# First layer of a fused attention and expert kernel: first w_in row blocks loaded among pair 3, seven column groups open at once, a narrow float16 warm-up

## Chip, cores, metric

One core of one Trainium2 chip. The metric is device time in microseconds (us) for one execution. Each kernel is compared with the kernel before by runs on the same chip in the same rounds.

## The reference, cut to what matters

```python
kv  = einsum('bhsd,bhse->bhde', k, v)           # 8 batches, 8 heads, 576 rows, 64 columns
out = einsum('bhsd,bhde->bhse', q, kv)
x   = out / sqrt(mean(out*out) + 1e-6) * g_norm # then (8*576) x 512
h   = x @ w_in                                  # 512 x 2048: the first layer
g   = h * (1 / (1 + exp(-1.702 * h)))           # the gate
y   = g @ w_out                                 # 2048 x 512: the second layer
```

## The kernel before

TensorE does the attention of batch b+1 between the matmuls of the two layers of tile b. Only for batch 0 is there nothing to hide behind. Its 8 heads are handled as four pairs. For each pair the kernel transposes q, forms the key-value product, multiplies the two ("out"), squares on ScalarE, sums on TensorE, takes ln and exp on ScalarE ("rs") and applies the factor on VectorE. That gives one of the four row blocks (ko) of xT. The first layer of tile 0 needs row block ko of xT and of w_in for its matmul (ko, fo); there are 16 column groups fo, and a group's sum stays in a PSUM buffer until all four row blocks are in.

```python
    GROUP = 6
    ...
    for c in range(1, NPAIR):                 # loads of batch 0, pairs 1 to 3
        for n in "qkv":
            early_load(n, 0, c, c + 1)
    load_w_in(0, 4, 0, 2)                     # column groups 0..3, row blocks 0 and 1
    load_w_in(0, 4, 2, KO)
    load_w_in(4, GROUP)
    load_w_in(GROUP, 10)
    load_w_in(10, FO)
    ...
    for _ in range(3):                        # warm-up of TensorE, float32
        nc.tensor.matmul(idle_ps, zeros[:, 0:P], zeros, start=True, stop=True)
    a0.q(0)
    busy(2)                                   # two idle 512-column matmuls
    a0.kv(0)
    ...
    a0.q(3)
    a0.kv(3)
    a0.sums(2)
    a0.apply(1)
    a0.out(3)
    a0.rs(2)
    a0.apply(2)
    busy(1)
    d0 = Hidden(0)
    for fo in range(4):
        d0.mm(0, fo, ...)
        if fo == 2:
            a0.ss(3)
            a0.apply(3)
    for ko in range(1, KO):
        for fo in range(4):
            d0.mm(ko, fo)
    for fo in range(4, GROUP):
        for ko in range(KO):
            d0.mm(ko, fo, ps_o, "o")
    for fo in range(GROUP):
        d0.gate(fo)
```

After this the other column groups run one by one, each through one of three buffers of the pool `ps_h`, and the second layer follows.

## Time and profile before

| what | value | where from |
|---|---|---|
| time, median of 3 | 287.08 us (286.64 to 287.28) | runs |
| span of the profiled run | 285.0 us | profile page |
| first matmul of the first layer | 14.24 us | TensorE timeline |
| last row block of xT ready | 16.78 + 0.75 = 17.53 us | VectorE timeline |
| second layer starts | 29.00 us | TensorE timeline |
| from there to the end | 285.0 - 29.0 = 256.0 us | the two rows above |

From 29 us on TensorE has no hole, so 256.0 us is what all later work costs, and a change of the first 29 us moves the end one for one. The lines are in the prediction below.

### The profile page before, as it was taken

To read this page: it belongs to the slowest core of one execution; us is meant where nothing else is said; L and a number is where in the kernel's file an instruction comes from. 1 tells how busy PE (TensorE), PEld (TensorE's weight loads), DVE (VectorE), ACT (ScalarE), POOL (GpSimd) and SP (SyncE) were. 2 spreads that over 40 slices of the span, in tenths; PEclk is the share of its full clock that TensorE was granted. 3 is DMA by queue.
4 is the path that set the end of the run, shared out by engine and by line. 5 is a ranking of instruction groups with operands and counts; after the bars stand their busy time and mean duration, and the time that the engine had idled before them with its cause. 6 is when DMAs were issued, how large, how long until landed. Compare 5 with 4: busy or idle time off the path is not lost.

```text
span 285.0 us, 4335 instructions
## 1 busy us (share of the span) xinstructions
PE 278.8 (98%) x1707; PEld 134.9 (47%) x1707; DVE 119.2 (42%) x231; ACT 156.2 (55%) x273; POOL 57.2 (20%) x82
## 2 busy tenths in 40 slices
PE   7899999999999999999999999999999999999995
PEld 3444554455445544554455445544454444444443
DVE  2650566527661657157713852286327400110001
ACT  2697439766575645574468536763666365016400
POOL 8931551111211121112011401130002100000000
PEclk9999999999999999999999999999999999999999
DMA  8999999999589356953798279925401410011022
GB/s 176 198 207 204 207 246 235 201 240 179 122 165 254 61 145 161 245 85 71 218 200 152 38 215 198 188 39 184 83 2 37 119 65 2 0 67 80 2 74 74
DMA packets 54070, 38.76 MB, mean 136 GB/s; under 512 B 31219, under 2 KB 50931, under 8 KB 53923
## 3 DMA queue, kind: packets, MB, share of 16 engines
q0 software_dynamic: 14960, 15.58, 33.5%
q1 hardware_dynamic: 38688, 22.39, 30.6%
q10 hardware_dynamic: 402, 0.52, 0.6%
q8 instruction: 13, 0.21, 0.3%
q14 instruction: 7, 0.05, 0.1%
HBM read 36.73 MB, written 9.44 MB: 162 GB/s over the span
## 4 chain that ended last, share of the span: by engine, by line
PE 93%; DMA 3%; POOL 3%; issue 0%; DVE 0%
PE hT L436 43%; PE o L473 42%; DMA w_in_sb<-in_moe_w_in_dram 3%; PE kvp L225 3%; PE outR L289 2%; PE oh L505 1%; POOL qraw L91 1%; POOL kraw L91 1%; POOL vbuf L91 1%; PE ss L337 1%; PE q L414 0%; PE outT L268 0%; PE outT L257 0%; POOL w_in_sb L168 0%; POOL ident L154 0%
## 5 line engine op out<-in xcount | busy, mean ns | idle before, releaser
L473 PE MATMUL o<-w_out_sb,gT 128*128 128x512 f16 x560 | 130.7, 379 | 0.0
L445 ACT ACTIVATE gT<-hT 128x512 f16<-128x512 f32 x144 | 84.7, 599 | 76.8 <-PE hT L436 76.5
L436 PE MATMUL hT<-xT,w_in_sb 128*128 128x512 f16 x512 | 116.5, 379 | 0.1
L436 PEld LDWEIGHTS <-w_in_sb 128*128 128x128 f16 x576 | 54.3, 98 | 63.1 <-DMA w_in_sb<-in_moe_w_in_dram 1.6
L473 PEld LDWEIGHTS <-gT 128*128 128x128 f16 x560 | 52.9, 98 | 56.4
L483 DVE COPY osb<-o 128x512 f32<-128x512 f32 x20 | 13.8, 690 | 62.3 <-PE o L473 62.3
L321 POOL TENSOR_TENSOR x<-xr,g_all 128x512 f16<-128x512 f32 x12 | 15.3, 1272 | 71.2 <-DVE xr L314 47.2
L216 DVE COPY kpad<-kraw 64x576 f16<-64x576 f16 x56 | 25.0, 446 | 1.7 <-DMA kraw<-in_k_dram 0.4
L300 DVE TENSOR_REDUCE sum<-sq 128x8 f32<-128x512 f16 x24 | 15.8, 679 | 19.9 <-ACT sq L297 19.9
L238 DVE CAST kvb<-kvp 64x128 f16<-64x128 f32 x28 | 8.1, 288 | 36.5 <-PE kvp L225 36.3
L314 DVE TENSOR_TENSOR xr<-outR,sum 128x512 f32<-128x512 f32 x24 | 15.5, 686 | 11.1 <-ACT sum L311 11.1
L112 POOL DMA_DIRECT2D kraw<-in_k_dram x16 | 10.0, 625 | 48.2 <-DVE kpad L216 42.3
L112 POOL DMA_DIRECT2D vbuf<-in_v_dram x16 | 9.7, 610 | 34.1 <-PE kvp L225 29.3
L321 DVE TENSOR_TENSOR x<-xr,g_all 128x512 f16<-128x512 f32 x12 | 15.2, 1267 | 0.7
L297 ACT ACTIVATE sq<-outR 128x512 f16<-128x512 f32 x24 | 13.6, 591 | 2.0 <-PE outR L289 1.6
L225 PEld LDWEIGHTS <-kpad 128*128 128x128 f16 x252 | 11.1, 98 | 6.5 <-DVE kpad L216 0.2
L436 PE MATMUL hT<-x_rem,w_in_sb 128*128 128x512 f16 x64 | 14.0, 379 | 0.0
L277 ACT ACTIVATE sq<-outT 128x512 f16<-128x512 f32 (+1 forms) x16 | 7.7, 481 | 11.0 <-PE outT L257 9.5
L483 ACT COPY osb<-o 128x512 f32<-128x512 f32 x15 | 8.7, 582 | 6.3 <-PE o L473 6.3
L310 ACT ACTIVATE sum<-sum,eps_t 128x16 f32<-128x16 f32 x12 | 3.7, 308 | 15.0 <-DVE sum L300 14.9
L225 PE MATMUL kvp<-vbuf,kpad 128*128 128x64 f16 x252 | 11.9, 193 | 0.0
L339 ACT ACTIVATE ln<-ss,eps_t 128x512 f32<-128x512 f32 (+1 forms) x16 | 9.4, 585 | 3.4 <-PE ss L337 3.4
(65 smaller groups left out, 140.7 us busy)
## 6 DMA issues: line engine op xcount, KB each, us to landing
qf<-in_q_dram SPq DMA_DIRECT2D x5, 1024.0 KB, 8.7
out_dram<-osb SPq DMA_DIRECT2D x10, 512.0 KB, 2.9
kraw<-in_k_dram POOLq DMA_DIRECT2D x12, 288.0 KB, 7.5
vbuf<-in_v_dram POOLq DMA_DIRECT2D x12, 288.0 KB, 5.4
w_out_sb<-in_moe_w_out_dram POOLq DMA_DIRECT2D x3, 512.0 KB, 14.8
out_dram<-osb SPq DMA_DIRECT2D x6, 192.0 KB, 5.6
qf<-in_q_dram POOLq DMA_DIRECT2D x1, 1024.0 KB, 12.2
out_dram<-osb SPq DMA_DIRECT2D x1, 1024.0 KB, 3.8
```

What stands on the lines that cost most here:

```text
L112: nc.gpsimd.dma_start(out=raw[n][l * PH : (l + 1) * PH, c0:c1, 0 : NH * D], in_=srcs[n][b].rearrange("(c l) (p j) d -> l p c (j d)", l=2, ...
L216: nc.vector.tensor_copy(out=kpad[r, c, :, l * D : (l + 1) * D], in_=kraw[r, c, 0 : NH * D].rearrange("p (j d) -> p j d", j=NH),)
L225: nc.tensor.matmul(self.kvp[:, c, :], kpad[:, c, j, :], vbuf[:, c, j * D : (j + 1) * D], start=(j == 0), stop=(j == NH - 1),)
L297: nc.scalar.activation(sq, t, AFT.Square)
L300: nc.vector.tensor_reduce(out=self.sum2[:, j % 2, :], in_=sq.rearrange("p (h d) -> p h d", h=H), op=ALU.add, axis=mybir.AxisListType.X,)
L314: nc.vector.tensor_mul(xr[:, i], self.o[j + i].rearrange("p (h d) -> p h d", h=H), s2[:, i, :].unsqueeze(2).to_broadcast([P, H, D]),)
L321: (nc.vector if i else nc.gpsimd).tensor_mul(self.x16[:, j + i, :].rearrange("p (h d) -> p h d", h=H), xr[:, i], g_all.unsqueeze(1).to_bro ...
L339: nc.scalar.activation(ln[:, 0:n], t[:, 0:n], AFT.Ln, bias=eps_t, scale=1.0 / D)
L436: nc.tensor.matmul(self.h[fo], w_in_sb[:, ko, fo * P : (fo + 1) * P], self.x[:, ko], start=(ko == 0), stop=(ko == KO - 1),)
L445: nc.scalar.activation(self.gT[:, fo, :], self.h[fo], AFT.Gelu_apprx_sigmoid)
L473: nc.tensor.matmul(os[mo], gT[:, fo, mo * P : (mo + 1) * P], w_out_sb[:, fo, :], start=(fo == 0), stop=(fo == FO - 1),)
L483: copy(osb[:, mo, :], os[mo])
```

## The change

Its intent is to start the first layer earlier. Small pieces of w_in are to be there when the first row block of x is, seven groups instead of six give TensorE work while it waits for the last row block, and the warm-up no longer needs a float32 tile. Later slots are moved to suit. The core of the diff:

```diff
-    GROUP = 6
+    GROUP = 7
...
-    zeros = const.tile([P, SM], F32)
-    nc.vector.memset(zeros, 0.0)
...
             early_load(n, 0, c, c + 1)
-    load_w_in(0, 4, 0, 2)
-    load_w_in(0, 4, 2, KO)
-    load_w_in(4, GROUP)
-    load_w_in(GROUP, 10)
-    load_w_in(10, FO)
+            if c == NPAIR - 1 and n != "v":
+                ko = "qk".index(n)
+                load_w_in(0, 4, ko, ko + 1)
+    load_w_in(0, 4, 2, 3)
+    load_w_in(4, 6, 0, 3)
+    load_w_in(6, GROUP, 0, 3)
+    load_w_in(0, GROUP, 3, KO)
+    load_w_in(GROUP, 9)      # and (9, 11), (11, 13), (13, FO)
...
-    for _ in range(3):
-        nc.tensor.matmul(idle_ps, zeros[:, 0:P], zeros, start=True, stop=True)
+    for _ in range(64):
+        nc.tensor.matmul(
+            idle_ps[:, 0:D], kvb[1][:, 0, :], kvb[1][:, 0, 0:D], start=True, stop=True
+        )
+    busy(4)
...
     a0.q(3)
-    a0.kv(3)
-    a0.sums(2)
     a0.apply(1)
-    a0.out(3)
-    ...
+    d0 = Hidden(0)
+    d0.mm(0, 0)
+    a0.sums(2)
+    a0.rs(2)
+    d0.mm(0, 1)              # and (0, 2), (0, 3)
+    for fo in range(4):
+        d0.mm(1, fo)
+    a0.apply(2)
+    a0.kv(3)
+    d0.mm(2, 0)
+    a0.out(3)
+    for fo in range(1, 4):
+        d0.mm(2, fo)
+    a0.ss(3)
+    a0.apply(3)
+    for fo in range(4, GROUP):
+        for ko in range(KO - 1):
+            d0.mm(ko, fo, ...)
+    for fo in range(GROUP):
+        d0.mm(KO - 1, fo)
...
     (cut and told in words from here on)
-    (k, v, w_out of tile 1 in turn)     -> (w_out blocks 8 to 11 before v)
-    (key-value products of tile 1 at steps 27, 28, 42, 43)  -> (36, 37, 46, 47)
-    (outputs at 32, 35, 50, 53)         -> (41, 43, 52, 53); loads of tiles 2 and 3 a little later,
     and the first matmuls of the later tiles take the first four groups in the order 0, 3, 1, 2
```

More of the change, by code (lines that the diff above doesn't have):

```diff
@@ L177 @@
             early_load(n, 0, c, c + 1)
-    load_w_in(0, 4, 0, 2)
-    load_w_in(0, 4, 2, KO)
-    load_w_in(4, GROUP)
-    load_w_in(GROUP, 10)
-    load_w_in(10, FO)
+            if c == NPAIR - 1 and n != "v":
[6 more added lines that the diff above has]
+    load_w_in(GROUP, 9)
+    load_w_in(9, 11)
+    load_w_in(11, 13)
+    load_w_in(13, FO)
     nc.scalar.preload_act_table_set("natural_log_exp_and_others")
@@ L450, in dense @@
         if group and t:
-            order = [(ko, fo) for part in (range(4), range(4, group)) for ko in (0, 1) for fo in part]
+            order = [(ko, fo) for part in ((0, 3, 1, 2), range(4, group)) for ko in (0, 1) for fo in part]
             order += [(ko, fo) for ko in range(2, KO) for fo in range(group)]
@@ L592 @@
     a0.q(3)
+    a0.apply(1)
+    d0 = Hidden(0)
[3 more added lines that the diff above has]
+    d0.mm(0, 1)
+    d0.mm(0, 2)
+    d0.mm(0, 3, ps_a, "att")
+    for fo in range(4):
+        d0.mm(1, fo)
+    a0.apply(2)
     a0.kv(3)
-    a0.sums(2)
-    a0.apply(1)
+    d0.mm(2, 0)
     a0.out(3)
-    a0.rs(2)
-    a0.apply(2)
-    busy(1)
-    d0 = Hidden(0)
-    for fo in range(4):
-        d0.mm(0, fo, *((ps_h, "hT") if fo < 3 else (ps_a, "att")))
-        if fo == 2:
-            a0.ss(3)
-            a0.apply(3)
-    for ko in range(1, KO):
-        for fo in range(4):
-            d0.mm(ko, fo)
+    for fo in range(1, 4):
+        d0.mm(2, fo)
+    a0.ss(3)
+    a0.apply(3)
     for fo in range(4, GROUP):
-        for ko in range(KO):
-            d0.mm(ko, fo, ps_o, "o")
+        for ko in range(KO - 1):
+            d0.mm(ko, fo, *((ps_o, "o") if fo < 6 else (ps_a, "att")))
+    for fo in range(GROUP):
+        d0.mm(KO - 1, fo)
     for fo in range(GROUP):
@@ L616 @@
     load_w_out(4, 8)
-    for c in (0, 2):
-        load_half("k", 1, c, c + 2)
-        load_half("v", 1, c, c + 2)
-        if c == 0:
-            load_w_out(8, 12)
-        else:
-            load_w_out(12, 14)
-            load_w_out(14, FO)
+    load_half("k", 1, 0, 2)
+    load_w_out(8, 10)
+    load_w_out(10, 12)
+    load_half("v", 1, 0, 2)
+    load_half("k", 1, 2, NPAIR)
+    load_half("v", 1, 2, NPAIR)
+    load_w_out(12, 14)
+    load_w_out(14, FO)
     load_q(2, nc.gpsimd)
@@ L660 @@
                 at2(9 + 3 * c, of(1, "q", c))
-                at2((21, 21, 33, 33)[c], of(1, "pack_k", c))
-                at2((27, 28, 42, 43)[c], of(1, "kv", c))
-                o = (32, 35, 50, 53)[c]
+                at2((21, 21, 38, 38)[c], of(1, "pack_k", c))
+                at2((36, 37, 46, 47)[c], of(1, "kv", c))
+                o = (41, 43, 52, 53)[c]
                 at2(o, of(1, "out", c))
                 if c == NPAIR - 1:
-                    at2(46, load_kv, 2)
-                at2((38, 46, 56, 59)[c], of(1, "ss", c))
-                at2((38, 46, 56, 59)[c], of(1, "apply", c))
+                    at2(48, load_kv, 2)
+                at2((45, 48, 56, 58)[c], of(1, "ss", c))
+                at2((48, 51, 56, 60)[c], of(1, "apply", c))
         elif b < B:
@@ L679 @@
             if t + 2 < B:
-                at1(f0, load_q, t + 2)
-                at1((10 if t == 1 else 9) + 4, load_kv, t + 2)
+                at1(12 if t == 1 else f0, load_q, t + 2)
+                at1((11 if t == 1 else 9) + 4, load_kv, t + 2)
             for c in range(NPAIR):
                 at1(f0, of(b, "pack_k", c))
-                at1((10 if t == 1 else 9) + c, of(b, "kv", c))
+                at1((11 if t == 1 else 9) + c, of(b, "kv", c))
             at2(6, nc.scalar.preload_act_table_set, "natural_log_exp_and_others")
```

## The prediction

> **What bounds the kernel now.** I read the page first (busy shares), then the chain that ended last, then the first 30 us engine by engine, then the DMA landings there.
>
> ```profile
> PE 278.8 (98%) x1707; PEld 134.9 (47%) x1707; DVE 119.2 (42%) x231; ACT 156.2 (55%) x273; POOL 57.2 (20%) x82
> ...
> PEclk9999999999999999999999999999999999999999
> DMA  8999999999589356953798279925401410011022
> ```
>
> TensorE is busy 98% of the span, and the DMA engines are full for the first quarter. Busy is not the same as useful, so the chain, limited to the first 30 us, decides:
>
> ```profile
> 8.01 0.72 POOL w_in_sb L168
> 8.73 7.80 DMA w_in_sb<-in_moe_w_in_dram
> 16.53 0.05 issue
> 16.58 5.48 PE hT L436 x24
> 22.06 0.12 PE outT L268 x4
> 22.17 6.99 PE hT L436 x32
> ```
>
> The chain follows a load of w_in until 16.53, and then nothing but TensorE. From 22 us on its pieces hold 0.216 us per 512-column matmul with no hole worth naming. As a check I count the matmuls after 29.0 us, where the second layer starts: 560 x 0.216 (second layer) + 512 x 0.216 (first layer of tiles 1 to 8) + about 21 us of small ones (252 key-value products at 0.029, 96 row products at 0.056, sums, transposes, the split last tile) = 252.5 us. The chain needs 281.6 - 29.0 = 252.6 us for them. So **only what happens before 29 us can be won**, or new stalls created after it. The TensorE timeline there:
>
> ```profile
> 13.79 0.39 PE L257 MATMUL outT<-qT,kvb 128*128 128x512 f16 x1
> 14.02 0.38 PE L560 MATMUL idle<-kvb 128*128 128x512 f16 x1
> 14.24 0.82 PE L436 MATMUL hT<-xT,w_in_sb 128*128 128x512 f16 x3
> 14.98 0.38 PE L337 MATMUL ss<-sq,ones 128*128 128x512 f16 x1
> 15.20 6.86 PE L436 MATMUL hT<-xT,w_in_sb 128*128 128x512 f16 x29
> 21.89 0.28 PE L268 MATMUL outT<-qT,kvb 128*128 128x64 f16 x4
> ```
>
> The first layer of tile 0 starts at 14.24 and its first 32 matmuls (8 column groups x 4 row blocks) are issued by 21.89. They and one sum need 33 x 0.216 = 7.13 us; they got 7.65. About 0.5 us is lost. The list of waits says to what (columns: us in total, times, longest):
>
> ```profile
> PEld L436 <- DMA w_in_sb<-in_moe_w_in_dram: 1.6, 4, 0.6
> ```
>
> And ScalarE beside it:
>
> ```profile
> 15.40 0.69 ACT L339 ACTIVATE ln<-ss,eps_t 128x512 f32<-128x512 f32 x1
> 16.11 0.63 ACT L345 ACTIVATE rs<-ln 128x512 f32<-128x512 f32 x1
> 16.76 1.28 ACT L445 ACT_TABLE_LOAD   x1
> 18.06 3.77 ACT L445 ACTIVATE gT<-hT 128x512 f16<-128x512 f32 x7
> 22.09 0.60 ACT L445 ACTIVATE gT<-hT 128x512 f16<-128x512 f32 x1 [0.27 <-PE hT L436]
> ```
>
> The last normalised block (xT of pair 3) is ready at 17.53, the gate table follows at once, and by 22.09 the gates wait for TensorE and not the other way.
>
> **DMA landings.** From the issue times and the latencies asked one issue at a time: q, k, v of pair 3 land at 11.45, 12.2 and 12.9; the w_in pieces at 14.2, 16.5, 17.5, 20.05 and 23.8. In steady state a 144 KB piece takes 0.75 us and 256 KB about 1.3 us (some 200 KB per us). The POOL timeline also shows that issue number n stands until issue n-8 has landed (the second key half waits for the second w_in piece, the third w_out piece for the last w_in piece), so eight loads are in flight at most.
>
> [...]
>
> **The change part by part.**
>
> Warm-up: three float32 matmuls (5.06 us, ending near 6.5) become 64 narrow ones[...] and four wide ones[...], starting 0.2 us earlier since one memset of 0.48 is gone.[...] The key-value product of pair 0 waits for the cast of v, which ends at 7.59 because v lands at 6.9. So this part is worth 0.
>
> Loads: two pieces of 128 KB come before k and v of pair 3, about 0.65 us each. k of pair 3 lands near 12.9, v near 14.3; the pieces land near 12.1, 13.5, 15.0 (row block 2), 16 and 16.5 (groups 4 to 6), 17.5 to 18 (row block 3 of all seven).
>
> TensorE order, with the durations above (ln 0.69, rs 0.63, square 0.59, apply 0.75, product to kvb 0.29, 0.38 from a matmul's start to its result). Until the transposes of pair 3 at 11.96 all is as before. Then: xT0 ready 12.56, so row block 0 starts at 12.62; its four matmuls and the sum of pair 2 end at 13.8. xT1 is ready at 14.20 (rs ends 13.41, apply 0.75), so row block 1 runs 14.26 to 15.12: **0.45 us stall**. Key-value of pair 3: 15.12 to 15.4, and its copy to kvb follows apply of pair 2 (14.76 to 15.51) on VectorE: 15.6 to 15.9. Row block 2 starts with xT2 at 15.57; the output of pair 3 at 15.93; three more to 16.8. Square 16.35 to 16.94, sum 16.99, ln to 18.11, rs to 18.76, apply to 19.55. Meanwhile 9 matmuls of groups 4 to 6; group 5 takes the buffer of that sum and waits for ln: 18.16, **0.3 us stall**. Row block 3 starts at 19.6, 7 x 0.216 to 21.11, group 7 to 21.98. Before: 21.89. So **the front is a tie, +0.1 us**: the first layer starts 1.6 us earlier, but the last block of x comes 2.0 us later (19.55 against 17.53), because the output of pair 3 now stands behind eight matmuls and two loads.
>
> Gates: table load 18.78 to 20.06, then one per 0.48 us (the spacing in the group above). Gate 7 ends at 20.06 + 7 x 0.48 + 0.60 = 24.0. Group 10 needs the buffer of group 7 (three buffers), and TensorE would be there at 21.98 + 0.12 + 2 x 0.864 = 23.83. **Stall 0.2 to 0.3.** The smaller pieces of w_in take away the wait of under 0.1 at 23.8. Start of the second layer: 29.0 + 0.1 + 0.25 - 0.1 = 29.25.
>
> Later slots of tile 0: the w_out pieces for blocks 8 to 11 come before v, so key-value products move from step 27 to 36. Walking through the 64 steps: v lands near 37.2 and is used at 38.1; w_out 12 to 13 lands at 41.3 as now and is used near 42.4; the second normalised output of tile 1 ends within 0.2 us of its use. All just fit: 0. The moved loads of tiles 2 and 3: 0.
>
> Sum: +0.25 us, that is 287.3.
>
> **The rivals.** (1) *The stalls vanish and the earlier start is kept.* With no stall the same work from 12.3 ends at 20.3 rather than 21.9: at most -1.6. But w_out 14 to 15 lands at 42.7 now and is used at 43.3, in a stream of loads that is full from the start, so some 0.6 to 0.9 is all that can be kept: about 286.3. For it speaks that the later slots were all moved back relative to the loads, which is only needed if TensorE gets ahead of them. Against it, the chain of pair 3 worked out above. (2) *Loads take over*: the small pieces run below 200 KB per us, or v of pair 3 lands a microsecond later; each 0.1 us of that goes straight into the last xT and into the end: 288. The before has one such skew (256 KB landing in 2.3 us). (3) *A later slot stalls*: key-value of tile 1 before v is there, 0.3 to 0.8 us: 287.8. (4) *Warm-up fails*:[...] some 0.3 us of transposes and products longer, 287.4.
>
> **Range and chances.** My sum gives 287.3, rival 1 286.3; I give the sum somewhat more weight but not all, because the moved slots look measured: 287.0. The three runs of before spread over 0.6 us, and the stalls are known to 0.3 each: 286.0 to 287.9. 2% is 5.7 us; all that can be won is 1.6, and nothing here adds 5, so within 2% at 0.98, faster 0.005, slower 0.015.
>
> **What would show it right or wrong.** Right: first hT matmul near 12.6; stalls before row block 1 and row block 3; last xT of tile 0 near 19.5; table load near 18.8; gates back to back until group 10 and a short wait there; second layer from 29.0 to 29.5; no hole after. Wrong: last xT before 18.5, or a second layer that starts before 28.5 (rival 1); a wait for w_in or v of over 0.3 us in the front (rival 2); a hole between 36 and 47 us (rival 3); narrow matmuls or transposes at twice their duration after 6.5 us (rival 4).

The sum of the forecast came to +0.25 us, that is 287.3: +0.1 for the front, +0.25 for the gate wait (put at 0.2 to 0.3), -0.1 for the smaller pieces of w_in, 0 for the warm-up and for the later slots. The marks stand for what no profile of the kernel before showed: the durations of the new warm-up's matmuls and the end of the warm-up that followed from them, an allowance for the narrowest w_in piece (not a term of the sum), and how long rival 4 lasts. The 0 for the warm-up rests on the cast of v (7.59) and on my estimate that the new warm-up is over by then; that ScalarE and VectorE work in program order is an assumption of the schedule. The first profile of the changed kernel has the 64 narrow matmuls 0.053 us apart, the four wide ones 0.43 apart, and the end of both at 6.58.

## The result, and the profile after

The changed kernel took 287.44 us (median of six, 287.18 to 289.17), the kernel before 286.96 (six runs). The ratio is 1.0023 with an interval of 1.0 to 1.0047. Repeated in five more rounds it was 287.37 against 286.93, ratio 1.0016 (1.0004 to 1.0028). The change costs about 0.45 us; that is within 2%.

The profile that came with the first result is of the slowest of the six runs, 289.17 us. Its page has a line that differs from the one of before (the clock granted to TensorE in tenths, 40 slices of 7.2 us):

```profile
PEclk9979999999999999999999999999999999999999
```

The third slice is at 7. The clock records say that it was half from 13.90 to 17.31 us. (Where the expectations below name times of the clock or of instruction packets, such as 14.14 to 17.55 or 14.6, these were counted from a zero 0.24 us earlier than that of the timelines; in the text all times have the zero of the timelines.) In the TensorE timeline of the same run seven 512-column matmuls take 3.1 us (14.04 to 17.16) instead of 1.5:

```profile
14.04 3.19 PE L440 MATMUL hT<-xT,w_in_sb 128*128 128x512 f16 x7
...
17.16 0.43 PE L378 MATMUL kv<-vbuf,kraw 96*64 96x64 f16 x12
```

The other five runs took 287.2 to 287.7, so this is not what the median is made of.

### The profile page after: what moved, and what is told of

It reads as the page before. It is cut to its first block, busy times and chain, and to the rows that moved or that the text cites. A ratio compares the mean times of both kernels' runs of the same rounds, so it can differ in the third digit from the quotient of the medians.

```text
span 287.4 us, 4460 instructions
## 1 busy us (share of the span) xinstructions
PE 280.9 (98%) x1768; PEld 137.5 (48%) x1768; DVE 119.0 (41%) x230; ACT 155.9 (54%) x273; POOL 61.0 (21%) x88
## 4 chain that ended last, share of the span: by engine, by line
PE 91%; ACT 4%; DMA 2%; POOL 1%; issue 0%; DVE 0%
PE hT L440 42%; PE o L477 41%; PE kvp L229 3%; DMA vbuf<-in_v_dram 2%; PE outR L293 2%; ACT gT L449 1%; PE oh L509 1%; PE ss L341 1%; ACT ln L343 1%; ACT sq L281 1%; POOL qraw L91 0%; ACT L449 0%; ACT rs L349 0%; POOL kraw L91 0%; PE q L418 0%; PE outT L261 0%
## 5 line engine op out<-in xcount | busy, mean ns | idle before, releaser
L440 PE MATMUL hT<-xT,w_in_sb 128*128 128x512 f16 x512 | 118.5, 383 | 0.3 <-ACT gT L449 0.2
L440 PEld LDWEIGHTS <-w_in_sb 128*128 128x128 f16 x576 | 55.0, 98 | 63.9 <-issue 3.4
## 6 DMA issues: line engine op xcount, KB each, us to landing
w_out_sb<-in_moe_w_out_dram POOLq DMA_DIRECT2D x4, 256.0 KB, 10.3
```

The costliest lines, as they stand in the source:

```text
L440: nc.tensor.matmul(self.h[fo], w_in_sb[:, ko, fo * P : (fo + 1) * P], self.x[:, ko], start=(ko == 0), stop=(ko == KO - 1),)
```

## The experiments

Twelve kernels ran, each with five rounds. All gave correct results. Each call has its own runs of the kernel before (medians 286.93, 286.88, 286.93) and was on another chip: e1 to e4, e5 to e8 and e9 to e12 ran together. A difference of 0.2 to 0.4 us between a kernel and e1_again of another call is therefore a hint, which its profile has to bear out; where I could, I read it from the profiles. The table has landmarks from every profile. "Front" is the start of the second layer; "rest" is the span minus it.

| kernel | time, median (range) | ratio to before | first kv product | first-layer start | last xT | front | rest |
|---|---|---|---|---|---|---|---|
| before | 286.96 | 1 | 7.64 | 14.24 | 17.53 | 29.00 | 256.0 |
| changed, first profile (half clock) | 287.44 | 1.0023 | 7.67 | 13.26 | 21.63 | 31.41 | 256.0 |
| e1_again | 287.37 (287.22 to 287.68) | 1.0016 | 7.52 | 13.18 | 19.83 | 29.61 | 256.0 |
| e2_old_warm | 287.62 (287.12 to 288.23) | 1.0022 | 7.87 | 12.84 | 19.85 | 29.63 | 256.0 |
| e3_warm_only (half clock) | 287.64 (287.30 to 288.37) | 1.0025 | 7.42 | 15.13 | 19.13 | 30.52 | 256.0 |
| e4_kv_early (half clock) | 287.19 (286.96 to 288.20) | 1.0013 | 7.73 | 13.59 | 20.51 | 30.44 | 256.0 |
| e5_wide_warm | 286.72 (286.66 to 287.17) | 0.9994 | 7.79 | 14.45 | 17.73 | 29.41 | 256.0 |
| e6_pair_first | 286.76 (286.44 to 288.25) | 1.0003 | 7.12 | 13.96 | 18.46 | 28.60 | 256.0 |
| e7_old_slots | 287.02 (286.83 to 287.29) | 1.0001 | 7.07 | 12.80 | 19.45 | 29.23 | 255.9 |
| e8_gate_buf | 287.07 (286.71 to 287.23) | 1.0000 | 7.76 | 12.73 | 19.74 | 29.19 | 256.1 |
| e9_all_three | 286.58 (286.28 to 287.87) | 0.9995 | 7.78 | 13.77 | 18.47 | 28.34 | 256.3 |
| e10_after_wide | 287.25 (286.56 to 288.12) | 1.0003 | 7.47 | 12.60 | 20.56 | 30.35 | 256.1 |
| e11_group6 | 287.80 (287.50 to 288.08) | 1.0027 | 7.36 | 13.21 | 19.86 | 30.02 | 256.0 |
| e12_more_instr | 287.41 (287.06 to 287.80) | 1.0013 | 8.17 | 15.06 | 18.27 | 29.66 | 256.0 |

Two readings come before the single runs. First, the rest is 255.9 to 256.3 in all fourteen profiles: whatever these kernels gain or lose, they do it before the second layer. Second, the first key-value product starts anywhere from 7.1 to 8.2 us, in most profiles because the first v lands at different times from run to run. A single profile is therefore uncertain by some tenths.

### e1_again: the changed kernel once more

No edit.

> The changed kernel, unaltered, to get a second profile. In the first profile (289.17 us, when its other five runs took 287.2 to 287.7) the granted clock fell to half from 14.14 to 17.55 us. Theory 1 (the sum of stalls of my prediction): the typical run has no half-clock stretch, takes 287.4, the second layer starts between 29.2 and 29.7, the last xT of tile 0 is ready near 19.5, group 10 of the first layer waits 0.2 to 0.3 us for a gate. Theory 2 (half clock is the loss): every run of the changed kernel has a half-clock window after 7 us and without it would be at 286 or below; then the profile shows matmuls 0.43 us apart again.

The second profile has full clock from 6.77 us on. The first part of its page (busy us, share of the span, instructions of each engine) hardly differs from that of before, 98% for TensorE again, which is why the busy share is no help here:

```profile
PE 278.9 (98%) x1768; PEld 137.0 (48%) x1768; DVE 118.9 (42%) x230; ACT 155.9 (55%) x273; POOL 61.0 (21%) x88
```

Its TensorE timeline answers to the one of before in the prediction:

```profile
13.18 0.39 PE L440 MATMUL hT<-xT,w_in_sb 128*128 128x512 f16 x1 [0.66 <-DMA w_in_sb<-in_moe_w_in_dram]
...
13.62 1.67 PE L440 MATMUL hT<-xT,w_in_sb 128*128 128x512 f16 x7
15.22 0.38 PE L378 MATMUL kv<-vbuf,kraw 96*64 96x64 f16 x12
16.00 0.38 PE L440 MATMUL hT<-xT,w_in_sb 128*128 128x512 f16 x1 [0.40 <-DVE xT L355]
16.22 0.38 PE L261 MATMUL outT<-qT,kvb 128*128 128x512 f16 x1
...
17.28 0.38 PE L341 MATMUL ss<-sq,ones 128*128 128x512 f16 x1
17.50 4.92 PE L440 MATMUL hT<-xT,w_in_sb 128*128 128x512 f16 x20
22.25 0.28 PE L272 MATMUL outT<-qT,kvb 128*128 128x64 f16 x4
...
24.43 5.34 PE L440 MATMUL hT<-xT,w_in_sb 128*128 128x512 f16 x24 [0.17 <-ACT gT L449]
```

The first layer starts 1.06 us earlier than before (13.18 against 14.24). But the product of pair 3 (line L378) starts at 15.22 instead of 13.02, behind the eight matmuls, and so the mark of 32 first-layer matmuls, the four small ones at 22.25, comes 0.36 later than the 21.89 of before. The eight matmuls after that mark need 1.73 us and would leave TensorE free at 24.1; the next starts at 24.43, a hole of 0.33. The chain that ended last shows the two halves of this (start, length, what; before it was TensorE alone from 16.58):

```profile
17.28 0.39 PE ss L341
...
17.70 0.69 ACT ln L343
...
18.41 0.63 ACT rs L349
...
19.06 1.28 ACT L449
...
20.36 4.03 ACT gT L449 x8
...
24.43 5.34 PE hT L440 x24
```

From 17.70 to 24.39 the chain runs through ScalarE: ln, rs, table load, eight gates. What ends last in that stretch has changed from TensorE to ScalarE, because the sum of the last pair comes 2.3 us later (17.28 against 14.98). Most of this is a load: v of pair 3 lands at 14.75 in e1 and at 12.88 before, so 1.87 of the 2.20 us by which its product is later are the landing, and only 0.33 its place in the program. What follows: theory 1, the sum of stalls, describes the typical run; a half-clock stretch is an extra that single runs have.

### e2_old_warm and e3_warm_only: the warm-up in both directions

e2 is the changed kernel with the old warm-up (and its zeros tile); e3 is the kernel before with the new one.

```diff
# e2: on the changed kernel                    # e3: on the kernel before, the reverse
-    for _ in range(64): (64-column matmul)
-    busy(4)
+    for _ in range(3):
+        nc.tensor.matmul(idle_ps, zeros[:, 0:P], zeros, start=True, stop=True)
```

> The changed kernel with the old warm-up (a zeros tile and three float32 matmuls). Theory 1: the warm-up is worth nothing, so within 0.2 us of the changed kernel, 287.4. Theory 2: the narrow warm-up matmuls are what leaves the array in a state from which it falls back to half clock; with the old ones no run shows the 1.5 us longer time, median 286.5 to 287.2.

> The kernel before with the new warm-up alone. Theory 1: 287.0 as before, within 0.2. Theory 2 (narrow warm-up costs clock): 287.3 or more, or single runs 1.5 us longer than the rest.

e3 is a miss for theory 1: the warm-up alone costs the kernel before 0.7 us in the median. Two of its six runs (288.26 and 288.37) have a mean granted clock of 0.994, the sign of a half-clock stretch; the mean of the four others, 287.50, is still 0.5 above that of before (286.97). So something costs time at full clock. It shows in the DMA queues between 10.5 and 12 us (queue: packets, MB, share of 16 engines). First the kernel before, then e3:

```profile
q0 software_dynamic: 412, 0.30, 130.6%
```

```profile
q0 software_dynamic: 402, 0.29, 127.1%
q8 instruction: 1, 0.02, 4.0%
```

One packet of 16 KB on a queue of kind instruction: 4.0% of 16 engines over 1.5 us is 0.96 us of a single engine; the packet records have it from 10.75, 0.949 us long. The kernel before has the same packet at 14.41. The loads show what goes with it. In e3 k of pair 3 lands 1.63 us after q of pair 3 (11.20 and 12.83), where 0.7 to 0.75 is the usual step; v of pair 3 lands at 13.25. TensorE waits for it, 1.21 us against 0.62 us before (bracket at the end; before, then e3):

```profile
13.02 0.38 PE L374 MATMUL kv<-vbuf,kraw 96*64 96x64 f16 x12 [0.62 <-DMA vbuf<-in_v_dram]
```

```profile
13.39 0.53 PE L372 MATMUL kv<-vbuf,kraw 96*64 96x64 f16 x12 [1.21 <-DMA vbuf<-in_v_dram]
```

In the kernel before, the packet meets the second piece of w_in instead: 256 KB land 2.3 us after the piece ahead of them, where 1.3 is usual. That is the "skew" my prediction mentions without a cause. In twelve of the fourteen profiles the load that lands 2.0 to 2.6 us after the start of the first such packet is 0.6 to 1.5 us later than its usual step; the exceptions are the first profile of the changed kernel and e12 (about 0.2).

Why it moves: the queue's kind is all that the trace says of the packet; that it brings TensorE's instructions is a reading of mine, and so is the name "16 KB fetch" in the expectations below. Its counts and times agree with that reading: the page of each kernel with the 64 narrow matmuls has 14 such packets, that of every other kernel 13, and in the first ten profiles TensorE had executed 221 to 304 matmuls and weight loads when the first packet within the loads came, be it at 10.6 or at 15.4 us. The new warm-up has 136 of them (64 + 64 and 4 + 4) where the old shows as twelve; by that reading the packet comes earlier.

e2 also missed both expectations in part: 287.62, no better. Its packet comes at 14.72 and the first w_in piece lands at 12.23 instead of 13.13. From the first key-value product to the second layer its profile has 21.76 us against 22.09 in e1; but that product itself is 0.35 later (7.87), since the float32 matmuls held the first transposes until 6.96, 0.46 later than in e1. So the last xT is ready at the same time, 19.85.

### e5_wide_warm: few instructions, same length

```diff
-    for _ in range(3):                       # on the kernel before; zeros tile removed
-        nc.tensor.matmul(idle_ps, zeros[:, 0:P], zeros, start=True, stop=True)
+    busy(12)                                  # 24 instructions
```

> The kernel before with twelve wide float16 matmuls as its warm-up: cold time as long as the new one (12 x 0.43 = 5.1 us), no zeros tile, but 24 TensorE instructions instead of 136. The warm-up alone had cost 0.5 us (287.64 against 286.93), which I had put at 0. Theory A[...]: a 16 KB packet of kind instruction took 0.95 us on one DMA engine, at 14.6 us in the kernel before and at 10.8 to 11.7 with the narrow warm-up, where the key and value loads of pairs 2 and 3 queue behind it; with few instructions it goes back to 14 to 15 us, v of pair 3 lands at 12.9 and the time to 287.0. Theory B (narrow matmuls or the missing memset leave the clock worse): 287.5 as with the narrow ones or single runs with a half-clock window.

286.72, ratio 0.9994 (0.9981 to 1.0007): the loss of e3 is gone, with the same missing memset and float16 operands as in e3. The packet is at 15.38, and the wait for v of pair 3 is back:

```profile
13.23 0.38 PE L372 MATMUL kv<-vbuf,kraw 96*64 96x64 f16 x12 [0.68 <-DMA vbuf<-in_v_dram]
```

Theory A stands: what the narrow warm-up cost the kernel before goes with the place of the instruction packet. (e5 changes the width and the number of the matmuls at once; what singles out the packet is the late k in e3 and the wait for v, 0.59 us longer there than before, which is the loss.) No run of e5 had a lower clock. The two medians in the expectation differ by 0.71; 0.5 is the difference at full clock. The 0.43 us per matmul in the expectation is the spacing of the four wide ones in the first profile of the changed kernel.

### e12_more_instr: only the number of instructions

```diff
     a0.q(0)
-    busy(2)            # on the kernel before, warm-up unchanged
+    narrow(22)         # 22 matmuls of 64 columns
...
-    busy(2)
+    narrow(16)
```

> The kernel before, its warm-up kept, with the four wide idle matmuls around the first key-value product replaced by 38 narrow ones of the same total time: 68 more TensorE instructions. Theory A (fetch position): the 16 KB fetch moves from 14.6 to 11.5 to 12.7 us, k or v of pair 3 or the first w_in piece lands up to 0.9 us late, 287.2 to 287.6. Rival (the narrow warm-up cost something else, such as clock or memset): fetch position is harmless, 286.9.

287.41 and none of the six runs below 287.06, as theory A expects, but the profile does not bear it out. The packet came at 12.98, later than I had said, and met only the first w_in piece; from the first key-value product to the second layer it took 21.49 us (before: 21.36). Its excess lies ahead of that, in a v that landed later (the product starts at 8.17). This run is inconclusive.

### e4_kv_early and e6_pair_first: where pair 3 stands

e4 moves the product of pair 3 ahead of row block 1. e6 moves it ahead of row block 0 too, with the sum of pair 2 first, and loads q, k, v of pair 3 before any w_in.

```diff
# e4                                   # e6
     d0.mm(0, 3, ps_a, "att")               a0.q(3)
+    a0.kv(3)                          +    a0.sums(2)
+    d0.mm(1, 0)                       +    a0.rs(2)
+    a0.out(3)                         +    a0.kv(3)
-    for fo in range(4):                    a0.apply(1)
+    for fo in range(1, 4):                 d0.mm(0, 0)
         d0.mm(1, fo)                  +    a0.out(3)
     a0.apply(2)                            (row blocks 0 and 1)
-    a0.kv(3)                               a0.apply(2)
     d0.mm(2, 0)                       +    a0.ss(3)
-    a0.out(3)                              (row block 2)
+    a0.ss(3)                               a0.apply(3)
     (cut here)                             (cut here)
```

> The changed kernel with the key-value product of pair 3 put before row block 1 instead of after it, and its output and sum accordingly earlier; loads unaltered. Theory 1 (the last xT is late because that product stands behind eight matmuls): last xT ready near 18.6 instead of 19.5, 0.5 to 0.8 us faster than the changed kernel, some 286.7. Theory 3 (v of pair 3 lands so late that its place in the program is irrelevant, loads bind): the product starts after 15 us in either order and the time stays within 0.2 us of the changed kernel.

> The changed kernel with q, k and v of pair 3 all loaded before w_in (the first row blocks right after), and the product and output of pair 3 put before row blocks 0 and 1. Theory 1 (the early w_in pieces and the place of pair 3 make the last xT late): last xT ready near 18.0 instead of 19.8, second layer from 28.0 to 28.7, 286.2 to 286.7. Rival: the first layer then waits for w_in as in the kernel before, last column groups late, 287.0 or more.

e4 gained 0.2 us in the median (287.19 against 287.37), less than expected; five of its runs are at 286.96 to 287.35 and the profiled one fell to half clock, so its last xT cannot be compared. By its numbers theory 3 is the one that came true: v of pair 3 landed at 15.28, the product started at 15.83, and the time stayed within 0.2 us. e6 has the last xT at 18.46 instead of 19.83, the second layer at 28.60 instead of 29.61, and a median of 286.76. The product of pair 3, now early in the program, still starts as soon as v has landed (13.34, against 14.75 in e1):

```profile
13.38 0.38 PE L377 MATMUL kv<-vbuf,kraw 96*64 96x64 f16 x12 [0.37 <-DMA vbuf<-in_v_dram]
```

That landing is 1.41 us earlier and the last xT 1.37, so the gain comes with the order of the loads; the place in the program alone is what e4 shows. From the sum of pair 3 to the mark of 32 matmuls TensorE has no wait,

```profile
16.12 5.34 PE L439 MATMUL hT<-xT,w_in_sb 128*128 128x512 f16 x24
```

and only the gate wait is left after it (the next 32 matmuls take 7.34 us, where e8 needs 7.07). Two of e6's six runs (288.25 and 288.08) have the lower clock, which is why its ratio is 1.0003. What follows: the early w_in pieces and the place of pair 3 together cost the changed kernel about 0.6 us (287.37 - 286.76; 0.8 with the means of full-clock runs, 287.41 and 286.60). The seven groups and split row blocks are not to blame; e6 has them.

### e7_old_slots: the later slots and loads as before

```diff
-  kv at (36, 37, 46, 47), out at (41, 43, 52, 53), ...   # on the changed kernel
+  kv at (27, 28, 42, 43), out at (32, 35, 50, 53), ...   # and the load order, all as before
```

> The changed kernel with the load order after the front and all later slots of tiles 0 to 2 as in the kernel before. Theory 1 (the moved slots are worth 0): 287.4 within 0.2. Rival: the old slots stall where the new ones do not, 287.7 or more; or the new ones cost, 287.1 or less.

The rest is 255.9 us with the old slots and 256.0 with the new: they are worth 0 with this front. The median is 0.35 lower than that of e1, outside my 0.2, so by the time alone the rival (287.1 or less, the new slots cost) came true; in its profile the first key-value product starts at 7.07, 0.45 earlier than in e1, and from there to the second layer it took 22.16 us against 22.09. I cannot say whether the old order of later instructions has a part in that or only the time at which the first loads landed in those runs.

### e8_gate_buf: the wait for gate 7

```diff
                 for ko in range(KO):
-                    hid.mm(ko, fo)
+                    hid.mm(ko, fo, *((ps_o, "o") if t == 0 and fo == 10 else (None,)))
```

> The changed kernel with column group 10 of tile 0 in a buffer of the other pool, free since gate 4. Theory 1: the wait of group 10 for gate 7 (0.33 us in the second profile) goes, second layer 0.3 earlier, 287.1. Rival: group 11 then waits for the same gate or the w_in piece binds there, 287.4.

287.07, 0.3 less than e1. The hole is gone: from the mark of 32 matmuls to the second layer the profile has 7.02 us (22.17 to 29.19) against 7.36 in e1 (22.25 to 29.61), and the TensorE timeline has 32 matmuls in one piece where e1 has 8 and 24:

```profile
22.28 7.07 PE L440 MATMUL hT<-xT,w_in_sb 128*128 128x512 f16 x32
```

### e11_group6: without the seventh group

```diff
-    GROUP = 7
+    GROUP = 6
-    load_w_in(6, GROUP, 0, 3)
```

> The changed kernel with six column groups open instead of seven. Theory: the last xT stays at 19.8, and three matmuls (0.65 us) that filled the wait for it now come after it, while the gate wait of 0.33 goes: 287.6 to 287.9. Rival: the seventh group fills nothing that would be idle and only makes the gate wait: 287.1.

287.80, 0.4 more than e1. The last xT is unmoved (19.86), and TensorE now stands before it:

```profile
19.91 3.18 PE L439 MATMUL hT<-xT,w_in_sb 128*128 128x512 f16 x14 [0.64 <-DVE xT L354]
```

0.64 us is the three matmuls. The second layer starts 0.41 later than in e1 (30.02 against 29.61). So the seventh group is worth 0.4 us net here: it fills a wait that the rest of the change has made.

### e10_after_wide and e9_all_three: the repairs

e10 is the changed kernel with `busy(12)` as its warm-up. e9 is e6 with that warm-up and with the buffer of e8.

> The changed kernel with twelve wide matmuls as warm-up and nothing else altered. Theory (fetch): the 16 KB fetch goes back to 14 to 16 us, the first piece of w_in lands near 12.3 instead of 13.1, no half-clock window; 287.0 to 287.2, since the late last xT and the gate wait stay. Rival: the warm-up costs nothing here because that late xT hides it, 287.4.

> The changed kernel with the three repairs together: pair 3 before w_in and its product early (as the kernel of that name), twelve wide matmuls as warm-up, column group 10 in the free buffer. In all ten profiles so far the span minus the start of the second layer is 255.9 to 256.1, so only that start counts. Theory: second layer at 28.0 to 28.4, 286.0 to 286.4, no run with a half-clock window. Rival (loads cap it): w_out blocks 12 to 15 land at 41.7 and 43.1 whatever the front does, TensorE waits for them in steps 48 to 52, and the time stays at 286.5 or above.

e10 gave 287.25 (286.56 to 288.12), hardly less than e1. The packet went back to 14.57 as expected, but in the changed kernel something urgent is loading then too. In the profiled run, the slowest of the six, it met row block 2 of w_in, which landed at 16.68, 2.0 us after the v ahead of it (14.69) where 128 KB usually take 0.65:

```profile
16.73 0.39 PE L440 MATMUL hT<-xT,w_in_sb 128*128 128x512 f16 x1 [1.30 <-DMA w_in_sb<-in_moe_w_in_dram]
```

e9 has the front at 28.34, within the expected range, and its best runs are at 286.28 to 286.40, half a microsecond under before. But the rest has grown to 256.26. In its chain the first key-value product of tile 1 waits for v (landed at 37.57), a block of w_out (43.01) and a sum take a little more:

```profile
37.63 0.08 issue
37.71 0.42 PE kvp L228 x9
...
43.02 0.03 issue
43.05 0.38 PE o L476
...
45.37 0.30 PE ss L340
```

The wait for v is what e6 does not have: of e9's lead of 0.26 us over e6 at the second layer, 0.03 is left at 46.75 us. So the loads begin to cap a faster front, as rival 1 said. The expected 286.0 to 286.4 was missed. And e9 had one run at lower clock (287.87) and one at 287.63 without: median 286.58, ratio 0.9995 (0.997 to 1.002). No kernel is shown to beat the one before.

### The half-clock stretch

Where a profile has it, it lasts 3.41 us and starts 6.83 us after the clock first went to full (before: the clock records begin, at full, at 6.05; first profile: at 7.07). The second half of these 6.83 us is a window in which TensorE waits for loads. Busy time of the engines in that window and the next, changed kernel, first profile (columns: stretch, length, then busy time and instruction count of PE, PEld, DVE, ACT, POOL; clock, DMA share, GB/s):

```profile
10.49:13.90 3.41, 2.34 (x41) 1.28 (x41) 1.86 (x4) 2.67 (x6) 3.00 (x5) 1.00 1.24 180
13.90:17.31 3.41, 3.41 (x14) 1.06 (x14) 1.50 (x2) 1.65 (x3) 3.32 (x5) 0.50 1.31 171
```

and e1, which kept its clock:

```profile
10.18:13.59 3.41, 2.46 (x41) 1.32 (x41) 2.10 (x5) 3.17 (x6) 2.29 (x5) 1.00 1.24 189
```

The other two that fell (e3, e4) had 2.20 and 2.10 us of TensorE work in that window, and the kernel before had 2.65. But e10 kept its clock through a later window with 2.27:

```profile
15.62:19.04 3.42, 2.27 (x9) 0.89 (x10) 0.17 (x1) 1.21 (x2) 2.27 (x4) 1.00 1.40 197
```

So little work in that window goes with the fall, and a fixed limit on busy time as the profile counts it does not explain it. Counting runs with a mean clock of 0.993 or 0.994: 6 of 45 runs of the kernels with the 64 narrow matmuls, 2 of 61 of those without (one of 33 of the kernel before, one of six of e9). That is a hint that the narrow warm-up makes the fall more frequent; with such counts it is not shown.

## Why the prediction was right or wrong

The time on record was 287.0 with a range to 287.9; it came out at 287.44. Its own sum, 287.3, was nearer than the number I made of it.

**Only what is before 29 us counts: right.** The rest is 256.0 us before and after, and within 0.3 in every experiment.

**The front is a tie, with an earlier start and a later last xT: right in mechanism, mis-sized by 0.3.** I had the start at 12.62, the last xT at 19.55, the 32-matmul mark at 21.98; e1 has 13.18, 19.83 and 22.25, and a second layer at 29.61 where I had 29.25. The term that was off is the landing of the first w_in piece, 12.1 in my list and 13.1 in e1, where the 16 KB packet (11.08 to 12.02) comes just ahead of it: it lands 1.58 us after q of pair 3, and 128 KB usually take 0.65. It delays the sum of pair 2 from about 12.95 (implied by my 15.51) to 13.40 and with it xT of pair 2 from 15.51 to 15.95. Where that piece landed at 12.23 (e2) the start is at 12.84. The 0.45 us stall before row block 1 shows as 0.28 in e2 and is absent in e1, where row block 0 came late enough; the stall of group 5, put at 0.3, is there: the 20 matmuls from 17.50 to 22.25 need 4.32 us and got 4.75, and the first matmul of group 5 stands until 18.43, just after ln ends at 18.39 (0.28), the rest being the wait for the last xT. The product behind "eight matmuls and two loads" is right too, but the loads weigh more than the matmuls: that e6 moves both and gains 0.6, and e4 the program alone and gains 0.2, shows the cause.

**The gate wait, 0.2 to 0.3: right.** 0.33 in e1; taking it away gains 0.3 (e8).

**The warm-up is worth 0: wrong.** This is the step that failed. I followed the TensorE path only. There the warm-up does cost nothing, since the first key-value product starts at 7.52 in e1 and at 7.64 before; but in e1 the cast of v is done at 7.13, so the product stands behind the transposes, which the warm-up held until 6.50, and two idle matmuls, and not behind v as I had said. What I left out is that with some 125 more instructions (4460 against 4335 on the two pages) the 16 KB instruction packet comes at about 11 us instead of 14.4, among the loads of pair 3. On the kernel before that costs 0.5 to 0.7 us (e3), and the same time in few instructions costs nothing (e5). In the changed kernel no gain shows when it is taken away: e2 loses it again ahead of the first product, and in e10's profile the packet meets another load that is waited for.

**The smaller w_in pieces save 0.1 at 23.8: not measured apart.** Later slots worth 0: right for the rest (e7). That at most eight loads are in flight is right, but it is the program's doing: the trace shows these loads taking eight semaphores in turn, and each from the ninth on waiting for the one of the load eight before it.

**The rivals.** Rival 1, which pulled my number down by 0.3, fell: its evidence was that the moved slots "look measured", and with the old ones the rest is the same (e7). Its figure for the cap was good, though: e9 shows the loads binding once the front is 0.7 us faster. Rival 2 happened in part, through a cause I had not seen: by the sign that I had set, a wait for w_in of over 0.3 us, it did (0.66 in e1). Its slow small pieces hardly show: the 96 KB piece, which writes 256 B per row, landed 0.54 us after the piece ahead of it in e1 and 0.28 in e9, where 200 KB per us make 0.48. Rival 3 did not happen. Of rival 4, half clock at the beginning, little shows (the first transposes take 0.55 us in e1 and 0.69 in the first profile, 0.45 before); half clock came at 14 us instead, in single runs.

**The chances and the range** held: +0.16% in the repeat.

Settled are the rest of 256 us, the place of pair 3 in loads and program together, the gate wait, the value of the seventh group, and the cost of the earlier instruction packet on the kernel before. Open stay what exactly lets the clock fall, why e7 is 0.35 us faster than e1, and what e12 shows.

## What to carry to other kernels

Starting a stage earlier gains nothing if its last input comes later: follow the last input through every engine and back to its load, and put the loads and the work that lead to it ahead of those that merely fill. In a stretch that waits for loads, count instructions as well as time; with some 125 more a 16 KB instruction packet came at 10.8 us here instead of 14.4 (e3), among loads that everything waited for. And take a second profile before explaining a first one that is slower than its own median.
